# DeltaNet attention with a gated feed-forward on one core: the first block inverse in blocks of 8, joined on TensorE

## The chip, the cores and the metric

One core of one Trainium2 chip. The metric is the device time of one execution in microseconds; the median of the runs is given. Lower is better.

## The reference

A DeltaNet layer (4 batches, 8 heads, 768 positions, head dimension 48) is followed by a feed-forward block of width 2048 on the 3072 x 384 result. Cut to what matters:

```python
k_n = k / (norm(k) + 1e-6)
for t in range(S):                      # 768 steps, per batch and head
    y[:, :, t] = q_t @ state
    v_old = state^T k_t
    state += beta_t * outer(k_t, v_t - v_old)
x = y.transpose(0, 2, 1, 3).reshape(3072, 384)
h = x @ w_in                            # 384 x 2048
out = (h / (1 + exp(-1.702 * h))) @ w_out
```

The weights `w_in` and `w_out` and the inputs come as they are generated; the weights are 64-bit floats and are turned into fp32 on the chip.

## The kernel before, in words

**Chunks and units.** The sequence is cut into chunks of C = 128. Within a chunk the recurrence is a unit lower triangular system: with G = -K K^T and a scaling by beta, the new values U solve (I + N) U = V, block by block. There are 24 units (a chunk of a batch each, the later ones two half chunks of 64); units 0 to 3 are chunk 0 of the four batches, units 4 to 7 the next chunk, and so on. A unit holds all eight heads.

**The first inverse.** `diagonal(n)` makes the 32 x 32 diagonal blocks of N of unit n in PSUM (`psD`), scales them by beta (`bT`) on VectorE and leaves them in `XBs`. A transpose on VectorE (32 x 32 streams) puts all 128 blocks of the four units on 128 lanes (`NT`, one block to a lane). `invert(0)` inverts on VectorE the two 16 x 16 halves of each block, row by row: fifteen times a product and a reduction (`P`, `YB`), then a scaling by `bI` and a transpose back to `XBs`. `merge` makes a 32 x 32 inverse out of the two 16s on TensorE: `psP` = G times the lower half, a mask (`upper`) on ScalarE, `psZ` = the upper half plus the transposed inverse times it.

**Hops.** With the 32 x 32 inverses a unit is solved in four blocks: `solve` (`psU` = inverse times V), `below` (its product with G is added to `psV` for the later blocks), `rest` (copy of the next block of `psV` into V). Two units go in turn, `hops(a, b)` with `together`, nine steps for a pair. Then `put_out` makes the outputs (`psY`), the state `ST` and the rows `xT` of the feed-forward; `copies` sends the rows that lie across partitions through `last` and DMAs to `xT`.

**Weights.** Each piece of raw 64-bit words is fetched by DMA to spare places (`raw`, gT tiles, TW, the not yet used parts of `w_out`) and converted by five VectorE operations and one on ScalarE, the clamp (`conversion`, line 253 on). `fill(us)` puts as many microseconds of such conversions into VectorE's program order as its argument says; `background` continues behind the sixth `w_out` piece with `invert(1)`, the full inverse of units 4 to 7 on VectorE (lines 647 to 731), and then the rest of `w_out`. `invert(1)` begins with `NT` times `bL`: NT comes from `load_diagonals` (blocks of G, written to DRAM by `send_blocks`, read back), bL from sixteen small DMAs on POOL's queue. Its result goes through DRAM (`Yd`) back to `XBs`.

**Order.** What goes through `vec`, `act`, `pe`, `pool`, `sync` and `other_queue` (POOL's DMA queue) keeps the order in which it stands in the program (line 139, the line that the profile names for nearly all); each engine runs its instructions in order. `warm(n)` puts n products of a constant on TensorE that nobody reads. The order around the change is written out by hand in lines 1423 to 1620: all four `gram(b)` (G of units 0 to 3), `run(invert(0))`, the scores (`scored`, `psQ`) of units 0 to 2, `merge` and hops of units 0 and 1, then `merge` and hops of units 2 and 3 with one step of `hidden` (three products `ph`) at each hop (`feed`), then 25 rounds of `fill(1.0)` and `feed` that also norm the keys of units 8 to 11 (`normalize_mixed`: `ssq`, `rn`), then `slot(n)` for units 3 on, the loop that has the rest of the time. Pieces of `w_in` are fetched in step with the work (`paced`: a copy of a value into the target makes the DMA wait for that value).

Of the kernel before, what the change touches and what calls it, by code (L numbers as in the profile page):

```python
# [8 lines left out]
F32 = mybir.dt.float32  # L9
# [9 lines left out]
def kernel(  # L19
# [31 lines left out]
    NB = C // BS  # L51
    HB = 2
# [35 lines left out]
    YB = cpool.tile([128, BS, BS], F32, name="YB")  # L88

# [280 lines left out]
    def background():  # L370

        converting = conversions()
        while ("out", order[HF - 2]) not in done:
            yield next(converting)
        yield from invert(1)
        done.add("inverse")
        yield from converting
# [46 lines left out]
    def normalize_first():  # L424

        tt, add = vec.tensor_tensor, ALU.add
        z = wk.tile([128, 4, B, H], F32, tag="ksq", name="z", bufs=1)
# [128 lines left out]
    def diagonal(n):  # L556
# [6 lines left out]
        for j in range(NP):  # L563
            for k in range(NB):
                t = slice(k * BS, (k + 1) * BS)
                for hh in range(2):
# [4 lines left out]
                    )  # L571
        for hh in range(2):
            vec.tensor_tensor(
                XBs[:, n, hh::2], ps[hh],
                bT[:, n * H + hh : (n + 1) * H : 2].broadcast_to([128, NP, BS]), op=ALU.mult,
            )

# [68 lines left out]

    def invert(c, b0=0, nb=B):
# [4 lines left out]
        bc = (bL[part, c - 1] if c else bI[part]).broadcast_to([np, BS, BS])  # L652
        tt, red = vec.tensor_tensor, vec.tensor_reduce
        if c > 0:
            tt(N, N, bc, op=ALU.mult)
            yield 1.2
# [30 lines left out]
        if c > 0:  # L687
            X1 = N[:, 0:HS, HS:]
            turned = halves(Y)[1].rearrange("p l i -> p i l")
            vec.tensor_copy(X1, turned)  # L690
            A = N[:, 0:HS, 0:HS]
            N10, Y0 = N[:, HS:, 0:HS], halves(Y)[0]
        for j, Q in ((0, 2), (2, 2), (4, 4), (8, 4), (12, 4)) if c > 0 else ():
# [8 lines left out]
        for i, Q in ((0, 4), (4, 4), (8, 4), (12, 2), (14, 2)) if c > 0 else ():  # L702
# [10 lines left out]
        if c == 0:  # L713
            vec.transpose(by_lanes(XBs), YS.rearrange("p j i -> p i j"))
            for b in range(B):
                inverse[b] = XBs[:, b]
            return
# [16 lines left out]
    def merge(pair, area, banks):  # L734

        XT, Pm = (
            [area[:, a + i * n : a + (i + 1) * n].rearrange("p (h k) -> p h k", h=H) for i in range(HB)]
            for a, n in ((0, H * BS), (HB * H * BS, H * BS // 2))
        )
        Z, HS = [inverse[X.n] for X in pair], BS // 2  # L740
        rows = [slice(k * BS, (k + 1) * BS) for k in range(NB)]
        for X, t in zip(Z, XT):
            vec.transpose(t.rearrange("p h k -> p (h k)"), X.rearrange("p h k -> p (h k)"))
        for X, x, m in zip(pair, Z, Pm):
            ps = banks[0][0].tile([128, H, HS], F32, tag=banks[0][1], name="psP")
            for h in range(H):
                for r in rows:
                    pe.matmul(
                        ps[r, h, :], lhsT=X.G[r, h, r], rhs=x[r, h, HS:], start=True, stop=True,
                        skip_group_check=True,  # L750
                    )
            act.activation(m, ps, ACT.Copy, scale=upper)
            yield
        for x, t, m in zip(Z, XT, Pm):
            ps = banks[1][0].tile([128, H, HS], F32, tag=banks[1][1], name="psZ")
            pe.matmul(ps, lhsT=ident, rhs=x[:, :, HS:], start=True, stop=True, skip_group_check=True)
            for h in range(H):
                for r in rows:
                    pe.matmul(
                        ps[r, h, :], lhsT=t[r, h, :], rhs=m[r, h, :], start=False, stop=True,  # L760
                        skip_group_check=True,
                    )
            act.copy(x[:, :, HS:], ps)
            yield

# [8 lines left out]
    class Step:  # L774
# [17 lines left out]
        def scores(self):  # L792
# [17 lines left out]
            for g in range(0, NP, 2):  # L810
                pool_, tag = (ps_seq, "seq") if g else (ps_big, "big")
# [33 lines left out]
        def below(self, blk, h, psR):  # L845
            r = slice(blk * BS, (blk + 1) * BS)
            for k in range(blk + 1, NB):
                u = slice(k * BS, (k + 1) * BS)
# [4 lines left out]

        def rest(self, blk, psR):
            u = slice((blk + 1) * BS, (blk + 2) * BS)
            act.copy(self.V[u], self.psV[u])

        def solve(self, blk, h, psU):
            r = slice(blk * BS, (blk + 1) * BS)
            pe.matmul(  # L860
                psU[r, h, :], lhsT=inverse[self.n][r, h, :], rhs=self.V[r, h, :],
                start=True, stop=True,
            )

        def solved(self, blk, psU):
            r = slice(blk * BS, (blk + 1) * BS)
# [422 lines left out]
    def together(solves, belows):  # L1289
# [4 lines left out]
        psRs = [bank("psR") if X.n >= B else None for X, blk in belows]  # L1294
# [91 lines left out]
    for blk in range(NB):  # L1386
        sync(out=bI[blk * NBH : (blk + 1) * NBH], in_=betas[:, 0, blk, :])
    pool.memset(YB, 0.0)
    pool.affine_select(
        out=YB, in_=YB, compare_op=ALU.not_equal, fill=1.0, base=0,  # L1390
        pattern=[[1, BS], [-1, BS]], channel_multiplier=0,
# [13 lines left out]
    for b in range(B - 1):  # L1405
        load(b, ((QP, q),), sync)
    warm(NW)
    normalize_first()
    vec.transpose(bT, bI)
    upper = cpool.tile([128, 1], F32, name="upper")  # L1410
    vec.tensor_reduce(
        upper, ident.rearrange("p (k o i) -> p k o i", k=NB, o=2)[:, :, 0], axis=AX.XY, op=ALU.add
# [8 lines left out]
    vec.transpose(NT.rearrange("p i k -> p k i"), by_lanes(XBs))  # L1421
    pool.tensor_copy(home(B)[0:1, 0, 0:1], XBs[0:1, B - 1, H - 1, 0:1])
    for n in range(B, 2 * B):
        load(n, ((KN, k),), sync)
    load(B - 1, ((QP, q),), sync)
    for b in range(HB):
        load_values(b, sync)
# [232 lines left out]
```

## Time and profile before

| | |
|---|---|
| median of 3 runs | 692.75 us (686.65 to 693.12) |
| the profiled execution, its own time | 683.09 us |
| its span, mean granted TensorE clock | 681.4 us, 0.991 |
| TensorE (PE) busy | 660.4 us, 97% |
| VectorE (DVE) busy | 479.5 us, 70% |
| ScalarE (ACT) busy | 233.6 us, 34% |
| GpSimd (POOL) busy | 269.4 us, 40% |

| place in the profiled execution | us from the span's start |
|---|---|
| first inverse on VectorE, with its transposes | 21.68 to 38.17 |
| `merge` of units 0 and 1, first `psP` | 38.74 |
| hops of units 0 and 1 | 45.47 to 64.8 |
| hops of units 2 and 3 | 78.66 to 97.1 |
| `load_diagonals` of units 4 to 7, issue | 86.17 to 89.72 |
| `invert(1)` on VectorE | 103.06 to 134.26 |
| first `psU` of the slot loop | 153.83 |

How to read it: times are microseconds from the span's start; busy shares are averages over the whole span, and TensorE's share counts the unread products of `warm` too. In the page's slices each of the 40 columns is 17 us and each digit the busy share in tenths. In the chain of waits each row is a start, a duration and what the end of the program was waiting for in that time.

### The profile page before, as it was taken

How to read it: one execution, taken by the hardware profiler on the slowest of the kernel's cores; microseconds unless marked ns; L12 is line 12 of the kernel's file. 1: busy time of each engine (PE TensorE's matmuls, PEld its weight loads, DVE VectorE, ACT ScalarE, POOL GpSimd, SP SyncE). 2: the span in 40 equal slices, each digit the busy share in tenths (PEclk: the TensorE clock that was granted, in tenths of full speed). 3: DMA queues.
4: the chain of work that ended last, by engine and by line, in shares of the span. 5: the costliest groups of instructions: out<-in, count | busy, mean ns of one | idle time of the engine just before them, and what ended most of it. 6: DMA issues, size and time to landing. Idle time of an engine off the chain costs nothing.

```text
span 681.4 us, 21731 instructions
## 1 busy us (share of the span) xinstructions
PE 660.4 (97%) x9290; PEld 563.4 (83%) x9290; DVE 479.5 (70%) x890; ACT 233.6 (34%) x571; POOL 269.4 (40%) x282
## 2 busy tenths in 40 slices
PE   9899899799999999999999999999999999999997
PEld 4766678566678998998998988988988988989997
DVE  4889799983788997996997996997976970200000
ACT  2558463632333233333333233233233233322120
POOL 4032844320286634635535526426305205105041
PEclk9799999989999999999999999999999999999999
DMA  9567575263334435335335244244231130100101
GB/s 174 105 165 175 128 218 99 44 155 81 83 74 92 96 63 109 79 67 104 71 67 116 67 90 88 66 86 79 62 78 19 38 75 2 30 2 6 26 0 24
DMA packets 149632, 54.61 MB, mean 80 GB/s; under 512 B 137824, under 2 KB 142656, under 8 KB 149536
## 3 DMA queue, kind: packets, MB, share of 16 engines
q1 hardware_dynamic: 146368, 46.62, 32.7%
q0 software_dynamic: 3168, 6.61, 3.7%
q8 instruction: 73, 1.20, 0.8%
q14 instruction: 23, 0.19, 0.1%
HBM read 38.37 MB, written 13.63 MB: 76 GB/s over the span
## 4 chain that ended last, share of the span: by engine, by line
PE 86%; DVE 6%; ACT 2%; DMA 2%; issue 2%; SPq 1%; DVEq 0%; ACTq 0%
PE po L139 34%; PE ph L139 32%; PE four L139 7%; PE psU L139 3%; PE psR L139 2%; PE psG L139 2%; DVE P L139 2%; DVE w_out L139 2%; PE ps_warm L139 1%; DVE YB L139 1%; DMA TW<-in_q_dram 1%; PE psQ L139 1%; SPq L139 1%; PE psV L139 1%; DVE NT L139 1%
## 5 line engine op out<-in xcount | busy, mean ns | idle before, releaser
L139 PE MATMUL ph<-xT,w_in 128*128 128x256 f32 x1152 | 261.0, 384 | 2.3 <-ACT gT L139 2.0
L139 PEld LDWEIGHTS ph<-xT,w_in 128*128 128x128 f32 x1152 | 215.9, 190 | 33.8 <-ACT gT L139 2.4
L1118 POOL TENSOR_TENSOR gT<-gT 128x512 f32<-128x512 f32 x80 | 103.0, 1298 | 97.9 <-ACT gT L139 66.0
L139 PE MATMUL po<-w_out,gT 128*128 128x192 f32 (+1 forms) x720 | 138.4, 347 | 0.0
L139 DVE TENSOR_TENSOR P<-NT,YB 64x8 f32<-64x8 f32 (+13 forms) x195 | 124.8, 640 | 5.8
L139 PEld LDWEIGHTS po<-w_out,gT 128*128 128x128 f32 x720 | 118.5, 190 | 11.0 <-ACT o L139 0.5
L139 ACT ACTIVATE gT<-ph 128x512 f32<-128x512 f32 x90 | 53.8, 598 | 154.8 <-PE ph L139 154.8
L139 DVE TENSOR_REDUCE YB<-P 64x4 f32<-64x8 f32 (+13 forms) x195 | 78.4, 402 | 6.7
L139 PE MATMUL po<-TW,gT 128*128 128x192 f32 x480 | 81.8, 328 | 0.0
L139 PEld LDWEIGHTS po<-TW,gT 128*128 128x128 f32 x480 | 78.1, 190 | 0.7
L984 POOL TENSOR_SCALAR_AFFINE_SELECT M<-M 64x512 f32<-64x512 f32 x40 | 29.1, 727 | 90.0 <-ACT M L139 88.8
L139 DVE TENSOR_TENSOR o<-o,late 128x192 f32<-128x192 f32 x20 | 6.6, 356 | 68.1 <-ACT late L139 67.9
L139 ACT COPY VU<-psU 32x384 f32<-32x384 f32 x96 | 45.2, 470 | 21.3 <-PE psU L139 14.9
L139 DVE TENSOR_TENSOR VU<-VU,psR 32x384 f32<-32x384 f32 x40 | 22.1, 553 | 36.6 <-PE psR L139 35.9
L400 POOL TENSOR_TENSOR rn<-ssq,half 128x8 f32<-128x8 f32 x12 | 22.3, 1858 | 52.6 <-DVE ssq L139 52.6
L139 DVE TENSOR_TENSOR VU<-VU,four 128x384 f32<-128x384 f32 x19 | 10.4, 548 | 46.1 <-ACT M L139 46.0
L109 POOL DMA_DIRECT2D KN<-in_k_dram x24 | 17.2, 716 | 58.4 <-PE four L139 56.7
L139 ACT COPY o<-po 128x192 f32<-128x192 f32 (+1 forms) x44 | 14.7, 334 | 74.6 <-PE po L139 72.5
L139 PEld LDWEIGHTS psU<-VU,XBs 32*32 32x32 f32 x1536 | 27.4, 105 | 13.5 <-issue 8.5
L139 PE MATMUL psU<-VU,XBs 32*32 32x48 f32 x1536 | 32.6, 203 | 0.3 <-ACT VU L139 0.2
L139 DVE TENSOR_TENSOR P<-NT 64x512 f32<-64x512 f32 (+7 forms) x45 | 30.5, 679 | 1.1
L139 DVE TENSOR_REDUCE NT<-P 64x32 f32<-64x512 f32 (+9 forms) x45 | 30.0, 668 | 1.5
(167 smaller groups left out, 752.1 us busy)
## 6 DMA issues: line engine op xcount, KB each, us to landing
VU<-in_v_dram SPq DMA_DIRECT2D x40, 96.0 KB, 2.8
out_dram<-o SPq DMA_DIRECT2D x40, 96.0 KB, 2.2
QW<-in_q_dram SPq DMA_DIRECT2D x76, 48.0 KB, 2.2
Kd<-KN SPq DMA_DIRECT2D x56, 64.0 KB, 2.2
late<-Kd SPq DMA_DIRECT2D x14, 256.0 KB, 2.8
KN<-in_k_dram POOLq DMA_DIRECT2D x30, 96.0 KB, 3.1
w_out<-in_moe_w_out_dram SPq DMA_DIRECT2D x7, 384.0 KB, 3.8
NT<-Nd SPq DMA_DIRECT2D x20, 128.0 KB, 2.7
```

Source lines behind the costliest of these rows:

```text
L109: dma(out=place(dst, n)[rows, :, 0:D], in_=src[b, :, t, :].rearrange("h p d -> p h d"),)
L139: return lambda *a, **kw: tc.keep_in_program_order(op(*a, **kw))
L400: nc.gpsimd.tensor_tensor(rn, ssq, half, op=ALU.pow)
L984: nc.gpsimd.affine_select(out=M, in_=M, compare_op=ALU.is_gt, fill=0.0, base=0, pattern=[[0, H], [1, CH]], channel_multiplier=-1,)
L1118: (engine or nc.gpsimd).tensor_tensor(o, a, b, op=op)
```

## The change

- `diagonal` keeps only the 8 x 8 diagonal blocks: the product with beta goes through a mask (`bG`, beta times `in_eighth`) and a reduction over the four blocks of 8 of each 32. `invert_first` inverts the 8 x 8 blocks, four on a lane, in seven steps of a product and a reduction on 256 elements a lane; `spread` puts them back on the diagonal of 32 x 32 blocks.
- `merge` joins three times: 8 to 16, 16 to 32 (each `psP`, a mask, `psZ`), and 32 to 64 (`wides`, in NT). For units 0 and 1 (`first`) VectorE does the masks and sums of the level 8 and the sums of the level 16, for units 2 and 3 ScalarE.
- A unit is solved in two blocks of 64: `solve(0)`, `below`, `solve(1)`.
- Order of units 0 to 3: `gram` of each unit between the scores; values of units 0 and 1 are fetched before the keys of units 4 to 7; units 2 and 3 are merged and solved between steps of `hidden` (`pass_`); their values, the last third of the third quarter of `w_in` and its fourth quarter are fetched behind `put_out` of unit 1; the first `w_out` pieces (`fetch_out(0..2)`) behind the mask of unit 3; `turn` and `gram` of units 4 to 7, `load_diagonals` and the DMAs of `bL` behind the solves of units 2 and 3. Most `warm` calls go. `fill` arguments between the first inverse and the 25 rounds sum to 37 us instead of 49.

```diff
+    def invert_first():
+        tt = vec.tensor_tensor
+        vec.transpose(lanes_N.rearrange("p i k -> p k i"), by_lanes(XBs[:, :, :, 0:E8]))
...
+        for i in range(1, E8):
+            P = wk.tile([128, NE, i, i], F32, tag="P", name="P", bufs=1)
+            tt(
+                P, eighths(lanes_N, i * E8, [[0, i], [1, i]]), eighths(lanes_Y, 0, [[E8, i], [1, i]]),
+                op=ALU.mult,
+            )
+            vec.tensor_reduce(
+                eighths(lanes_Y, i, [[E8, i]]), P, axis=AX.X, op=ALU.add, negate=True
+            )
+        tt(lanes_N, lanes_Y, bI.broadcast_to([128, BS, E8]), op=ALU.mult)
+        vec.transpose(packed.rearrange("p n k -> p k n"), lanes_N.rearrange("p j i -> p i j"))
...
+        for s in (E8, 2 * E8):
...
+            turn_blocks()
...
+                        pe.matmul(
+                            ps[r, h, :], lhsT=X.G[r, h, r], rhs=o[r, h], start=True, stop=True,
...
+                if k == 1:
+                    act.activation(m, ps, ACT.Copy, scale=upper)
+                elif first:
...
+                        pe.matmul(
+                            ps[r, h, :], lhsT=t[r, h, :], rhs=m[r, h, :], start=first, stop=True,
...
+                if first:
+                    vec.tensor_tensor(o, o, split, op=ALU.add)
+                else:
+                    act.copy(o, split)
...
-        def below(self, blk, h, psR):
-            r = slice(blk * BS, (blk + 1) * BS)
-            for k in range(blk + 1, NB):
-                u = slice(k * BS, (k + 1) * BS)
+        def below(self):
+            r, u = slice(0, CH), slice(CH, C)
+            for h in range(H):
                 pe.matmul(
                     self.psV[u, h, :], lhsT=self.G[r, h, u], rhs=self.U[r, h, :],
...
+        def solve(self, blk):
+            r = slice(blk * CH, (blk + 1) * CH)
+            psU = bank("psU")
+            for h in range(H):
+                pe.matmul(
+                    psU[r, h, :], lhsT=wides[self.n][r, h, :], rhs=self.V[r, h, :],
...
+    put_out(pair[1])
+    scaling = roots_second(areas)
+    next(scaling)
+    merging = merge(pair[2:], area, ((ps_seq, "seq"), (ps_seq, "seq")), False)
+    fetch_in(2, js=(2,))
+    for b in range(HB, B):
+        load_values(b, sync)
+    for j in range(KC):
+        fetch_in(3, js=(j,))
...
+    def pass_(us=2.2):
+        feed()
+        fill(us)
...
+    run(scored[3])
+    pair[3].select()
+    fetch_out(0, other_queue)
+    fetch_out(1, other_queue)
+    fetch_out(2, other_queue)
...
+    put_out(pair[3])
+    pass_()
+    gram(B + 2)
+    turn(B + 3)
+    pass_()
+    Nds.append(send_blocks(B + 2))
+    gram(B + 3)
+    load_diagonals(Nds + [send_blocks(B + 3)])
+    done.add("diagonals")
```

## The prediction

> **What bounds the kernel now.** I read the page's slices first, then the chain of waits and the timelines of the first 160 us (none of the edits lies behind that), then the windows with the granted clock.
>
> ```profile
> PE   9899899799999999999999999999999999999997
> DVE  4889799983788997996997996997976970200000
> ```
>
> TensorE is full from slice 9 (153 us) to the end, so what is behind 153 us moves as a block. VectorE is full from slice 1 to 8 and has room in slice 9 (a digit of 3). The chain of waits over the first 160 us (start, duration, what):
>
> ```profile
> 82.79 3.72 DMA w_out<-in_moe_w_out_dram
> ...
> 103.06 1.23 DVE NT L139
> ...
> 131.38 0.21 DVE rn L139
> ...
> 136.84 1.73 PE psQ L139 x32
> ...
> 143.32 10.52 PE po L139 x32
> 153.83 0.80 PE psU L139 x32
> ```
>
> From 82.79 on the chain is VectorE: weight conversions, then from 103.06 the inverse of units 4 to 7, between whose steps stand the key norms `rn` that ScalarE and, behind it, TensorE wait for; from 136.84 TensorE alone. Call X the start of that inverse (103.06) and P the first `psU` of the slot loop (153.83). The change is worth what P moves, if nothing queues up behind it.
>
> VectorE's first inverse and the tail (start, duration, instruction):
>
> ```profile
> 21.68 2.06 DVE L139 STREAM_TRANSPOSE NT<-XBs 128x1024 f32<-128x1024 f32 x1
> ...
> 28.47 0.37 DVE L139 TENSOR_TENSOR P<-NT,YB 128x200 f32<-128x200 f32 x1
> 28.87 0.36 DVE L139 TENSOR_REDUCE YB<-P 128x20 f32<-128x200 f32 x1
> ...
> 36.08 2.09 DVE L139 STREAM_TRANSPOSE XBs<-NT 128x1024 f32<-128x1024 f32 x1
> ...
> 133.09 1.17 DVE L139 TENSOR_TENSOR NT<-YB,bL 128x1024 f32<-128x1024 f32 x1
> ...
> 154.57 0.56 DVE L139 SCALAR_TENSOR_TENSOR w_out<-raw,w_out 128x384 f32<-128x384 f32 x1
> ```
>
> **First inverse.** It holds VectorE from 21.68 to 38.17, 16.5 us. Afterwards: two transposes of 128x256 (a quarter of 2.06, 0.5 each), seven pairs of product and reduction over 4 to 196 elements (the rows for 2 to 200 elements take 0.16 to 0.37 each, with 0.04 between: 3.9), a scaling of 256 (0.42). With a reduction of 0.42 more per unit ahead of it (the last counts) it runs from 22.1 to 27.4; two spreads of 0.42 end at 28.3. TensorE is later: four products `psG` of 1.8 (7.21 for four), two transposes and sixteen `psQ`, all now ahead of the joins, end at 31.8.
>
> **Joins and hops of units 0 and 1.** Each of the levels 8 and 16 is four groups of 0.73 (the rows `psP`, `psZ` x64), with VectorE or ScalarE between (0.25 to 0.4 and 0.1 to wake): 3.3 us a level. Third level and wide copies: first `psU` at 41.7 (45.5 now). The trace has no 64x48 product, 64x32 join or copy of 32x256; the nearest rows (16 `psU` of 32 rows 0.86, copies of 128x256 0.37 and of 32x384 0.47) bound a group by 0.4 and 0.9, some 3 us over the whole chain; I take 0.45, since as many rows go through in half as many products. Three steps (solve, below, solve) of two to three us, with copies of 0.47, replace nine hops that take from 45.5 to 64.8; ScalarE copies the last state at 53.6 instead of 69.9. Sixteen us sooner, but that is not yet P: X needs VectorE.
>
> **VectorE's stream up to X.** From 38.06 to 103.06 it holds 55 us of work and 10 of waits. Joins and wide copies now end there at 40.2; behind that lie the same conversions (48.4 by their rows: 2.74 for a piece of 512, 2.25 of 384, 4.1 of 768), two more pairs of transposes, norms: 55.6 us, so X = 95.8 without waits. The order of the changed kernel shows these:
> - The third `w_in` piece (2,2) and the values of units 2 and 3 are issued on SP's queue behind the `xT` transfers that wait for 53.6: x3 about 2.3, x4 2.5, landing 4.3 later: 62.7, against 59.8 at which VectorE reaches it: 2.9. The values land at 63.5, and TensorE, in order, stands at `psV` from 57.5.
> - A clamp on ScalarE stands behind the first `ph` groups: 1.7.
> - The first `raw` transfers are issued on POOL behind the mask of unit 3, which waits for `psQ` at 76: select 1.1, issue 0.6, landing 4.0: 83.2 against 79.9: 3.3. Now they are issued at 60.0.
> - Pauses that the profile calls issue, as now: 3.
> Sum 10.9: X = 106.7. The work of units 2 and 3 on TensorE follows the values at 63.5: two `psV` 1.5, eleven `ph` groups of 1.33 (14.6), the level-16 and wide joins 5.5, `psQ` 1.2, six solves and belows of 0.45, four transposes 2.4, `psY` with states 2.7, four `psG` 2.8: 33, so `psG` of unit 7 ends at 96.
>
> **What X also waits for.** The beta transfers `bL` and the diagonals are queued as follows today:
>
> ```profile
> 71.93 9.31 POOL L139 DMA_DIRECT2D bL<-in_beta_dram  x16
> 86.17 3.55 SPq L139 DMA_DIRECT2D NT<-Nd  x4
> ```
>
> Today both are early. Now `bL` comes behind POOL's `xT` of unit 3 (94.7): 94.7 + 9.3 + 3.7 to landing = 107.7. The diagonals: G of unit 7 at 96.6, sent 1.8, landed 3.3, loaded and landed 4.5: 106.3. Queued behind that wait on VectorE are the inverse, three of the four `rn`, and the second half of `w_out`. X = 107.7, 4.6 later than now.
>
> **From X to P.** The inverse takes 31 us as now, so it ends at 138.9. Three chains: (a) its way through DRAM (Yd 2.2, issue, XBs 4.1) ends at 145.3, 8.4 before P; (b) TensorE: the four norms now stand earlier in VectorE's order, the last at 125.6 instead of 131.5 though X is later, `psQ` at 128.6, and 15.0 from there (16.9 now, less a `ph` group that is moved ahead and a pause) `psU` at 143.6; (c) the second half of `w_out`: its last conversion ends 52.0 after X now (155.1); the moved norms and the two VU rows give 0.6 back, so 159.1. TensorE uses it 12 us after P (165.75 today), 10.7 us of slack. (c) is last: P moves by 159.1 - 165.75 = -6.6. VectorE is then late by some ten us in the slot loop and has 18 us of idle time from 154 to 198 to catch up.
>
> **The clock.** The warm-up products between 28 and 78 us are taken out. Windows now (start:end, length, busy PE, PEld, DVE, ACT, POOL, granted clock, DMA share, GB/s):
>
> ```profile
> 16.00:20.00 4.00, 2.51 (x154) 1.98 (x140) 2.26 (x6) 1.74 (x3) 0.00 (x0) 1.00 0.38 54
> 20.00:24.00 4.00, 3.82 (x120) 3.65 (x96) 3.20 (x6) 1.08 (x3) 0.17 (x1) 0.61 0.13 25
> 24.00:28.00 4.00, 4.00 (x42) 4.00 (x40) 3.45 (x17) 2.45 (x5) 0.00 (x0) 0.54 0.68 127
> ```
>
> After four us of small tiles with a pause of 1.49 the clock falls to half. There 64 `psD` took 0.81 instead of 0.76, but sixteen products of 128 columns 1.8 (`psG`) instead of 1.16 (`psQ`). The joins of 31 to 51 are such small tiles: at half clock the wide products between (`psQ`, `psV`, `psY`) cost 2 us more, the `ph` behind the pause at 57.5 another 2. Price 0 to 4 (a gain is excluded, the clock is full there today); I take 1.6, for nearest are the joins today, at a clock of 1.00 with warm-ups among them.
> The Trainium skill, page "TensorE: Matmul & The Clock Gate", section Part 1, says that the clock is halved after an idle window of about 3.4 us and full after one of the same length busy. By that, only the pause at 57.5 (six us) costs, 2 us; the trace agrees behind the pause of 3.59 us at 133.2 (clock 0.79 from 136 to 144), not at 20 us, where 1.49 sufficed.
>
> **Without cost:** the small masks reduced from `ident` (VectorE idles 2.98 before 4.48; if not, 0.5), the moved memset of YB (POOL idles 12.77 before 21.71), the other bank of `psQ`, fewer paced signs (SP is issuing throughout).
>
> Forecast: P moves by -6.6 + 1.6 = -5.0. The profiled execution took 683.09 (span 681.4 and 1.7 around), 9.7 under the median of the runs shown; so 678.1 there, 692.75 - 5.0 = 687.8 as a median.
>
> **Rivals.**
> B, no waits on VectorE: values, raws and diagonals arrive as it reaches them, X = 103. Then (c) gives -11: 681.7. For it: all three transfers that I find late are late by 3 us only, and the row of VectorE before X shows such waits of 3.45 and 1.68 already. Against: three queues would have to be wrong in the same direction.
> C, late diagonals: landing times at the upper end (`raw` shows 3.7 to 6.5), a TensorE pause of 1.0 to 1.5 of kind issue in each of four stages: X = 114 to 118. (c) says 0 to +4: 693 to 697. P decides from X = 114.3.
> D, slower: the clock stays at half from 31 to 96 us, because joins keep breaking the `ph` groups. Twelve groups cost 1.33 more each, 16; four `psY` 1.3 each, 5: X = 129, +15: 707. It loses over 1% from X = 121. For it: the windows above. Against: from 64 to 104 the clock is 1.00 today with `ph` among small tiles and no warm-ups behind 74.
> That the change doesn't do what it says is excluded by the order of the instructions: seven pairs, three joins, solves of 64.
>
> **How the numbers follow.** Forecast 0.48 (its own range -8 to -1: 685 to 692), B 0.27, C 0.14, D 0.11. A measurement tells about 1%, 6.9 us. Faster by more: B and a seventh of the forecast, 0.33; slower: D and some of C, 0.14; within: 0.53. The range from 680 (B with 2 us of spread in the runs) to 698 (C's end) leaves out D and a tenth of B.
>
> **What would show it.** Right: VectorE idle ahead of `NT` with `bL` or `NT` as the releaser, X near 108; first `psU` near 42; TensorE idle at `psV` near 60; the last `w_out` conversion just ahead of its `po`. Wrong: X at 103 or less (B), `ph` groups of 2.6 at a clock of 0.5 before 96 us (D), P behind 154, or TensorE waiting in the slot loop for VectorE, which I count at nothing.

## The result, and the profile after

The changed kernel is slower: 719.5 us as the median of 4 runs (713.58 to 725.34) against 690.0 (686.65 to 693.12), a ratio of 1.04 with a 95% interval of 1.0299 to 1.0501. The ratio leaves out the longest run, 725.34 us, which counts as slow. The forecast was 687.8. The profiled execution has a span of 717.1 us and a mean granted clock of 0.946, before 681.4 and 0.991: 35.7 us more. The medians differ by 29.5 only. The profiled execution of the kernel before (683.09 us) is one of its quickest: the forty runs of it in the experiments below took 682.65 to 694.84 us at a clock of 0.989 down to 0.969, the longer in the main the lower. Some six of the 35.7 us are thus a matter of which execution was profiled.

The slices of the changed kernel (17.9 us a column):

```profile
PE   8869899988899999999999999999999999999997
...
DVE  5542764789868899799699798797995991110000
...
PEclk9655679999999999999999999999999999999999
```

The clock of the kernel before (17 us a column):

```profile
PEclk9799999989999999999999999999999999999999
```

VectorE, full from the second slice in the kernel before, is at 2 to 7 tenths up to 143 us. The clock is near half in the second to fourth slice (18 to 72 us), where it stood at full from the third slice on. The chain of waits of the changed kernel (start, duration, what):

```profile
18.03 2.32 issue
...
37.19 2.13 issue
...
41.23 2.38 issue
...
45.51 1.58 issue
...
58.31 3.59 PE psU L147 x32
...
65.00 3.58 PE psV L147 x32
...
69.62 3.58 PE psU L147 x32
...
83.75 3.63 DMA VU<-in_v_dram
...
134.60 0.69 PE psG L147 x32
...
139.69 3.59 DMA KN<-in_k_dram
```

Up to 135 us it is no longer VectorE's chain: joins, solves and `ph` groups on TensorE follow each other, with pauses and one wait for values between. Then come the diagonals and the keys of unit 8 behind them on SP's queue, and X. (As in the prediction, X is the start of the inverse of units 4 to 7 and P the first `psU` of the slot loop.) On VectorE (start, duration, instruction, idle time before it):

```profile
59.59 1.10 DVE L147 SCALAR_TENSOR_TENSOR w_in<-w_out,w_in 128x768 int32<-128x768 int32 x1 [6.23 <-ACT w_in L147]
...
71.11 0.96 DVE L147 SCALAR_TENSOR_TENSOR w_in<-w_out,w_in 128x768 int32<-128x768 int32 x1 [7.24 <-ACT w_in L147]
...
144.56 0.55 DVE L147 TENSOR_REDUCE ssq<-ksq 128x8 f32<-128x384 f32 x1 [2.81 <-ACT ksq L147]
...
145.91 2.01 DVE L147 TENSOR_TENSOR NT<-NT,bL 128x1024 f32<-128x1024 f32 x1
```

X is 145.91, before 103.06, forecast 107.7. P, the first `psU` of the slot loop, is 184.11, before 153.76: 30.35 us later. The other 5.4 of the 35.7 come behind P: the next slot's `psU` stands 20.3 us after P, not 14.9. TensorE pauses there for a copy on ScalarE and for the last `w_out` conversion, and twelve `po` take 5.83 us and not 4.14:

```profile
190.64 0.27 PE L147 MATMUL psR<-VU,G 32*32 32x48 f32 x2 [1.60 <-ACT VU L147]
...
201.45 3.04 PE L147 MATMUL po<-w_out,gT 128*128 128x384 f32 x8 [1.27 <-DVE w_out L147]
```

One row each, from 28 us to P, first before, then after (columns as in the prediction):

```profile
28.00:153.76 125.76, 112.76 (x1904) 84.65 (x1901) 114.16 (x212) 69.54 (x174) 51.48 (x62) 0.99 0.61 142
```

```profile
28.00:184.11 156.11, 136.64 (x2195) 110.76 (x2194) 100.14 (x195) 68.20 (x175) 48.25 (x57) 0.79 0.49 107
```

TensorE's busy time has grown by 23.9 us although 12.8 us of warm-ups are gone; VectorE's has shrunk by 14. This stretch holds most of the loss, and the experiments are read by its sum.

### The profile page after: what moved, and what is told of

The parts are those of the page before. It is cut to its first block, busy times and chain, and to the rows that moved or that the text cites. A ratio compares the mean times of both kernels' runs of the same rounds, so it can differ in the third digit from the quotient of the medians.

```text
span 717.1 us, 22298 instructions
## 1 busy us (share of the span) xinstructions
PE 684.7 (95%) x9560; PEld 588.3 (82%) x9560; DVE 477.4 (67%) x902; ACT 234.0 (33%) x575; POOL 268.9 (38%) x282
## 4 chain that ended last, share of the span: by engine, by line
PE 85%; issue 5%; DMA 3%; DVE 3%; POOL 2%; SPq 1%; ACT 1%; POOLq 0%; ACTq 0%; DVEq 0%
PE ph L147 32%; PE po L147 29%; PE four L147 7%; PE psU L147 4%; PE psG L147 2%; PE psR L147 2%; PE psV L147 2%; PE psP L147 2%; DMA raw<-in_moe_w_out_dram 1%; DMA KN<-in_k_dram 1%; PE psZ L147 1%; SPq L147 1%; PE psT L147 1%; PE psQ L147 1%; PE psY L147 1%
## 5 line engine op out<-in xcount | busy, mean ns | idle before, releaser
L147 PE MATMUL ph<-xT,w_in 128*128 128x256 f32 x1152 | 264.1, 387 | 3.4 <-ACT TW L147 2.4
L147 PE MATMUL po<-w_out,gT 128*128 128x192 f32 (+1 forms) x720 | 140.3, 350 | 1.3 <-DVE w_out L147 1.3
L147 PEld LDWEIGHTS po<-w_out,gT 128*128 128x128 f32 x720 | 119.1, 191 | 13.6 <-DVE w_out L147 1.9
L147 DVE TENSOR_TENSOR P<-NT,YB 64x512 f32<-64x512 f32 (+24 forms) x180 | 118.7, 660 | 5.1
L147 ACT ACTIVATE gT<-ph 128x512 f32<-128x512 f32 x90 | 53.6, 597 | 152.6 <-PE ph L147 152.5
L147 DVE TENSOR_REDUCE YB<-P 64x4 f32<-64x8 f32 (+26 forms) x180 | 73.5, 408 | 6.2
L1091 POOL TENSOR_SCALAR_AFFINE_SELECT M<-M 64x512 f32<-64x512 f32 x40 | 29.5, 738 | 86.3 <-ACT M L147 85.0
L147 ACT COPY VU<-psU 32x384 f32<-32x384 f32 (+1 forms) x88 | 41.4, 470 | 18.2 <-PE psU L147 16.4
L147 DVE TENSOR_TENSOR VU<-VU,psR 32x384 f32<-32x384 f32 x40 | 22.1, 554 | 32.5 <-PE psR L147 31.8
L147 DVE TENSOR_TENSOR P<-NT 64x512 f32<-64x512 f32 (+14 forms) x52 | 32.3, 621 | 1.9 <-DVE NT L147 0.5
L147 DVE TENSOR_REDUCE NT<-P 64x32 f32<-64x512 f32 (+16 forms) x52 | 31.7, 610 | 1.8
L147 ACT COPY xT<-four 128x256 f32<-128x256 f32 (+1 forms) x40 | 13.1, 328 | 42.7 <-PE four L147 42.7
L147 PEld LDWEIGHTS psU<-VU,XBs 32*32 32x32 f32 x1280 | 15.7, 105 | 8.1 <-issue 6.4
```

What stands on the lines that cost most here:

```text
L147: return lambda *a, **kw: tc.keep_in_program_order(op(*a, **kw))
L1091: nc.gpsimd.affine_select(out=M, in_=M, compare_op=ALU.is_gt, fill=0.0, base=0, pattern=[[0, H], [1, CH]], channel_multiplier=-1,)
```

## The experiments

**The theories.** Theory 1: the half clock makes TensorE's chain long. Theory 2: the chain of joins and 64-row products is long in itself. Theory 3: late transfers. They were named ahead of the first run; Theories 4 (the order), 5 (VectorE's idle time), 6 (one chain in which all add up), 7 (VectorE runs dry) and 8 (the place of the diagonals) came as the earlier ones fell. All runs named below but one (timed once) were timed in rounds against the kernel before, whose medians lay between 690.5 and 692.0. The changed kernel's own runs span 12 us, so its variants between 713 and 724 us are hardly told apart by their times. What the text says of their parts is read from one trace of each.

### The four first suspects

Warm-ups back between joins and solves:

```diff
-    for _ in range(2 * HB + 2):
-        next(merging)
+    for _ in range(HB + 1):
+        next(merging), next(merging)
+        warm(NM)
...
+    warm(NM // 2)
```

> The changed kernel with unread warm-up products put back between the joins and the solves of units 0 and 1 (some 9 us of products at full clock, most of it in pauses of TensorE). Theory 1, the clock: the half clock from 24 to 76 us is what made the chain long; the granted clock is above 0.9 in most of 28 to 76 us, the 32 psU products take 2.0 us and not 3.65, the start of the inverse of units 4 to 7 moves from 145.9 to 128-134 us and the time falls by 12 to 18 us (to 702-708). Theory 2, the serial chain: the clock is higher, but the added products and the waits for VectorE and ScalarE eat it; the inverse starts at 140 us or later and the time falls by less than 6 us. Theory 3, late transfers: the inverse starts within 3 us of 145.9.

Measured: 722.7 us, ratio 1.0441 (1.0363 to 1.0518); X 153.99. The clock was 0.50 from 48 to 64 us all the same: 17.5 us of warm-ups (1.0 in the changed kernel) did not hold it. This tells nothing of the clock's price.

No warm-ups in the kernel before:

```diff
-    NW, NR, NA, NY, NM, NU = 80, 11, 3, 14, 8, 12
+    NW, NR, NA, NY, NM, NU = 80, 11, 0, 0, 0, 0
...
+        if n == 0:
+            return
```

> The kernel before without any warm-up products behind the first ones. Theory 1: the granted clock falls to 0.5 from about 24 to 60 us or longer here too, and the kernel is slower by 6 to 15 us. Theory 2: the joins and hops of 32 rows cost nearly the same at half clock (64 psD took 0.81 against 0.76 us), so the time stays within 3 us of the kernel before, whatever the clock. Theory 3: no change.

Measured: 685.1 us, ratio 0.9937 (0.9904 to 0.9971): a little faster than the kernel before, and so the fastest of all. The two profiled executions, with spans of 681.4 and 682.4 us, do not show it, since that of the kernel before had a clock that none of its timed runs reached. From 28 us to P of this kernel:

```profile
28.00:154.80 126.80, 113.68 (x1845) 90.02 (x1845) 113.95 (x210) 68.20 (x172) 52.54 (x62) 0.87 0.63 141
```

The clock is at half from 40 to 64 us. TensorE's own work grows from 98.9 (112.76 less 13.84 of warm-ups) to 113.7, just what the warm-ups had taken, and P moves by 1.0. In these two executions of the old order half clock and warm-ups cost the same.

Hops of 32 for units 0 and 1 in the changed kernel, without their third join:

```diff
+        if first:
+            return
...
-    for X in pair[:2]:
-        X.solve(0)
+    hop((p0, 0), None, 0)
+    for i in range(NB - 1):
+        hop((p1, i), (p0, i), 0)
+        hop((p0, i + 1), (p1, i), 0)
```

> The changed kernel, but units 0 and 1 are solved in hops over four blocks of 32, as before, and their third join (32 to 64) is left out; units 2 and 3 keep blocks of 64. Theory 2, serial products of 64 rows: the third join (four groups of 3.6 us and the wide copies, some 14 us in all) goes, first psU comes at 45 to 49 us instead of 58.2, nine hops take some 20 us against 20 for the solves and belows of 64, so the inverse of units 4 to 7 starts 8 to 14 us sooner and the time falls by 8 to 14 us (to 706-712) although the clock stays at half. Theory 1: the clock stays at half, hops at half clock are slow as well, and the time falls by less than 5 us. Theory 3: less than 3 us.

Measured: 718.4 us, ratio 1.0401 (1.0328 to 1.0473), X 145.51. First `psU` comes at 53.2, five us sooner, and nothing is left of it at X: the hops at half clock, with copies between, take back what the join gave. (A pair has eight hops in the program, not nine.) In the new order the size of the blocks is not it.

Transfers early (bL to the front of POOL's queue, values of units 2 and 3 ahead of the first inverse, `fetch_out(0..2)` behind `put_out` of unit 1):

```diff
+        load_values(b, sync)
     invert_first()
...
+    fetch_out(0, other_queue)
```

> The changed kernel with transfers moved ahead: the sixteen bL loads to the front of POOL's queue, the values of units 2 and 3 ahead of the first inverse, the first three w_out pieces right behind put_out of unit 1. Theory 3, late transfers: the waits for VU (3.7 us), raw (2.25) and what stands behind them go; the inverse of units 4 to 7 starts 6 to 10 us sooner and the time falls by 6 to 10 us. Theories 1 and 2: these waits were short and other waits of the chain take their place; the time falls by 0 to 4 us.

Measured: 719.5 us, ratio 1.0429 (1.034 to 1.0519), X 145.03. Taken alone, Theory 3 falls: with the values there, TensorE's products with them (`psV`) start at 89.5 us, no sooner (87.4 in the changed kernel).

### The two halves of the change

The first inverse in blocks of 8 with the joins to 32, put into the kernel before, its order kept:

```diff
-    run(invert(0))
+    invert_first()
+    spread(0, 2)
+    spread(2, 2)
...
+    for _ in range(2 * HB):
+        next(products)
```

> The kernel before with the first inverse in blocks of 8 and the joins 8 to 16 and 16 to 32 alone: its order of units 0 to 3, its hops of 32, its warm-up products and its early transfers stay. Theory 4, the order: what costs is that the new order puts VectorE (by the clamps on ScalarE) and the diagonals behind the whole TensorE chain of units 0 to 3; here they are ahead of it again, so the inverse of units 4 to 7 starts at 95 to 104 us, the loop at 146 to 155 and the time is from 8 us under to 2 us over the kernel before. Theory 2, the serial chain: two more joins of 64 small products for each pair, with the masks and pauses between, put the chain late in any order: the first hop comes at 50 us or later, units 2 and 3 6 us later again, and the time is 8 to 15 us over the kernel before.

The same with the third join and blocks of 64 for all four units:

```diff
+    run(products)
...
+        if i % 2 == 0:
+            together(*next(path))
...
+        if i == 6:
+            load_diagonals(Nds)
```

> As the run with the first inverse alone, and with the third join and the solves over blocks of 64 for units 0 to 3, still in the order of before; the wide inverses lie in NT, so that the diagonals of units 4 to 7 are loaded only behind the last solve of units 2 and 3. Theory 4: the inverse of units 4 to 7 starts at 100 to 112 us, the time is from 6 us under to 6 us over the kernel before. Theory 2: serial products of 64 rows make the chain long whatever the order: the inverse starts at 120 us or later and the time is 15 to 28 us over the kernel before, near the changed kernel.

The first of these two without warm-ups:

> The first inverse in blocks of 8 in the old order with hops of 32, without the warm-up products behind the first ones. Theory 4: the chain of TensorE of units 0 to 3 is not what VectorE waits for, so the half clock costs within 2 us of the same kernel with warm-ups, or gains up to 6 us as it did in the kernel before. Theory 1, the clock: 6 to 15 us slower than with warm-ups.

And the new order with the inverse of before, one join, and hops of 32 for all units:

```diff
-    invert_first()
+    run(invert(0))
...
-        for s in (E8, 2 * E8):
+        for s in (2 * E8,):
```

> The new order alone: the first inverse of before (two 16 x 16 halves on VectorE), one join to 32 and hops of 32 for all four units, in the order, with the transfers and without most of the warm-ups of the changed kernel. If the order costs by itself (Theory 4): the inverse of units 4 to 7 starts at 125 us or later and the time is 12 to 25 us over the kernel before. If what costs is the longer chain of joins and 64-row products on TensorE and the order only passes it on (Theory 2): the inverse starts at 105 to 115 us and the time is within 8 us of the kernel before.

Measured:

| | order of before | new order |
|---|---|---|
| inverse of before, hops of 32 | 690.0 | 721.5, ratio 1.0437 (1.0361 to 1.0514) |
| blocks of 8, hops of 32 | 704.2, 1.0224 (1.0133 to 1.0316) | 718.4, 1.0401 (1.0328 to 1.0473); 64 in units 2 and 3 |
| blocks of 8, blocks of 64 | 714.7, 1.0326 (1.0226 to 1.0426) | 719.5, 1.04 (1.0299 to 1.0501) |

Without warm-ups the left middle is 704.7 (1.0218, 1.013 to 1.0307): the same, so Theory 1 (6 to 15 us slower) fell there. Each half costs by itself, the order most, and they do not add: in the new order blocks of 8 and 64 change little either way. In the old order the inverse in blocks of 8 starts X at 122.84 and not 103.06. Theory 4 put it at 95 to 104 and fell there. In the old order Theory 2 came true: its 8 to 15 and 15 to 28 us over the kernel before were 12.2 and 22.6. But it put the order alone within 8 us of before and fell there.

What holds TensorE in the order alone, from 28 to 150 us (waited for, us in total, times, longest):

```profile
PE psU L147 <- ACT VU L147: 8.7, 8, 1.5
PE psV L147 <- DMA VU<-in_v_dram: 5.4, 1, 5.4
PE psP L147 <- DVE XBs L147: 5.0, 1, 5.0
```

In the old order `turn` and `gram` of units 4 to 7 and warm-ups stood between the hops; without warm-ups its list has a single wait of `psU` for VU, of 0.2 us. In the new order only two groups of transposes stand between the hops of units 0 and 1, and five of the seven steps behind the first wait for ScalarE's copy, 4.6 us in all.

### The sum from 28 us to P

All kernels by one sum: P less 28 us is TensorE's own work, its warm-ups and its idle time (us; busy time by the window of each kernel, warm-ups by their tile).

| kernel | P | own work | warm-ups | idle |
|---|---|---|---|---|
| before | 153.8 | 98.9 | 13.8 | 13.0 |
| before, no warm-ups | 154.8 | 113.7 | 0 | 13.1 |
| blocks of 8, old order | 175.1 | 112.7 | 18.3 | 16.0 |
| blocks of 8, old order, no warm-ups | 174.3 | 125.7 | 0 | 20.7 |
| blocks of 8 and 64, old order | 187.6 | 124.5 | 17.4 | 17.8 |
| order alone | 185.6 | 124.0 | 1.0 | 32.6 |
| changed | 184.1 | 135.6 | 1.0 | 19.5 |
| changed, dense warm-ups (below) | 179.5 | 115.4 | 20.7 | 15.4 |
| changed, no join to 16 (below) | 180.7 | 131.2 | 1.0 | 20.5 |

P's 30.35 us are 36.7 more of own work, 12.8 less of warm-ups, 6.5 more of idle time. Of the 36.7, `psP` and `psZ`, the joins, are 17.7 (12.9 + 12.3 against 3.1 + 4.4).

The kernel before without warm-ups is the fairer base, since it too ran in part at half clock, and its profiled execution (684.08) lies 1.0 under its median. Against it the order alone has 10.3 us more of own work, 1.0 of warm-ups and 19.5 of idle time; the changed kernel has 21.9, 1.0 and 6.4. So the order alone costs most in waits. By these sums the longer work of the changed kernel fills much of what is idle time there, which fits that the two halves do not add.

### What VectorE waits for, and what the clock costs

In every kernel so far X less VectorE's idle time from 30 us on was 91 to 98 us (before 103.06 - 5.3, changed 145.91 - 52.3). Theory 5 made the idle time the cause. The clamp taken off ScalarE for the pieces ahead of the inverse:

```diff
-        act.activation(p, p, ACT.Relu, scale=8.0, bias=low)
+        if "inverse" in done or "late" in done:
+            act.activation(p, p, ACT.Relu, scale=8.0, bias=low)
+        else:
+            ts(p, p, 896 * E1, 896 * E1, op0=ALU.max, op1=ALU.subtract)
+            ts(p, p, 8, None, op0=ALU.mult)
```

> The changed kernel with the clamp of every weight piece that is converted ahead of the inverse of units 4 to 7 done on VectorE in two operations (about 10 us more of work there), not on ScalarE. Theory 5, VectorE's idle time: in all kernels run so far the inverse starts at 91 to 98 us plus VectorE's idle time from 30 us on (5.3 us in the kernel before, 52.3 in the changed one), and some 28 of the 52 us are waits for clamps that stand in ScalarE's order behind TensorE's work. With those waits gone the idle time falls to 15-30 us, the inverse starts at 122 to 136 us, and the loop starts 4 to 12 us sooner, since TensorE itself still needs about 45 us from psG of unit 7 (135) to the loop; the time falls by 4 to 14 us. Rival (Theory 2 alone): VectorE then waits for the joins and for transfers at the same places, the inverse starts within 5 us of 145.9 and the time changes by less than 3 us.

Measured: 723.9 us, ratio 1.0512 (1.0438 to 1.0586), X 149.77. The clamp waits are gone and others stand in their place:

```profile
75.15 0.95 DVE L147 TENSOR_REDUCE TW<-squares 128x16 f32<-128x768 f32 x1 [10.08 <-ACT squares L147]
...
118.15 0.36 DVE L147 TENSOR_SCALAR w_out<-raw 128x384 int32<-128x384 int32 x1 [9.40 <-DMA raw<-in_moe_w_out_dram]
```

VectorE's idle time shows how late TensorE's chain is; it is not the cause. Theory 5 falls.

Dense warm-ups between joins, solves and belows of units 0 and 1:

```diff
+        warm(ND)
...
+        warm(ND // 2)
```

> The changed kernel with so many warm-up products between the joins, solves and belows of units 0 and 1 (about 80 of 512 columns, 20 us at full clock, 40 at half) that the clock should stay full; it is meant to price the clock and not to be fast. Read: the time from the first psP to the last psY of unit 1 (34.3 to 78 us in the changed kernel, 44) less the busy time of the warm-ups. Theory 1: the rest is 24 to 30 us, since psU, psV and the 64-row joins take 2.0 us and not 3.6 and psY, psQ half. Theory 2: 34 us or more is left, in pauses and waits between the steps. If the clock stays at half all the same, warm-ups cannot hold it between these products and the question stays open.

Measured once: 713.2 us, 6.3 under the changed kernel's median and next to its lowest run (713.58), so that the time alone shows no gain. A window of this kernel and two rows of its chain of waits:

```profile
40.00:80.00 40.00, 38.42 (x917) 25.77 (x906) 19.35 (x35) 16.24 (x42) 3.95 (x7) 1.00 0.16 38
```

```profile
61.30 1.06 PE psU L147 x16
...
70.19 1.99 PE psU L147 x32
```

The clock is 1.00 from 40 to 80, and 32 `psU` take 1.99 us, not 3.58. By the expected reading, 36.1 to 76.4 us less 19.0 of warm-ups leaves 21.2, under the 24 to 30 of Theory 1 (the warm-ups also fill pauses). In the sum TensorE's own work falls by 20.2 us and the warm-ups cost 19.7: the clock is the largest single price in the changed kernel, and buying it back with warm-ups costs as much. With the clock held the joins take 20.1 us in all, not 25.2. What P gained, 4.6, is mostly idle time that they filled (19.5 to 15.4).

The join to 16 left out:

```diff
-        for s in (E8, 2 * E8):
+        for s in (2 * E8,):
...
-    for _ in range(2 * HB + 2):
+    for _ in range(2 * HB):
```

> The changed kernel without the join 8 to 16 of all four units (its two times four groups of products, masks and sums are left out, so the inverses lack those blocks). Theory 2, a serial chain: the join's length goes from the path twice: first psU at about 48 to 51 us and not 58.2, units 2 and 3 another 3 to 6 us, so psG of unit 7 is 10 to 16 us sooner, the inverse of units 4 to 7 starts 8 to 16 us sooner, the time falls by 8 to 16 us. Theory 3 or 5 with VectorE bound elsewhere: less than 4 us.

Measured: 714.2 us, ratio 1.0369 (1.0282 to 1.0456). The 5.3 us under the changed kernel are neither the 8 to 16 of Theory 2 nor clear of the runs' spread. First `psU` comes at 50.8, 7.4 sooner; X at 144.25, P at 180.73. Of 7.4 us in units 0 and 1, 3.4 reach P: TensorE then waits 5.5 us for the values of units 2 and 3.

Conversions moved to where VectorE idled in the old order:

```diff
+    fill(6.5)
...
-    fill(4.0)
+    fill(1.0)
```

> The kernel with the first inverse in blocks of 8 in the old order (hops of 32), with 9.5 us of weight conversions moved from behind the hops to where VectorE idled 8.05 and 9.06 us there: behind the first inverse and between the joins to 32. Theory 5: VectorE's idle time ahead of the inverse falls from 28.8 to about 15 us and the inverse starts at 108 to 116 us and not 122.8; the diagonals (landed at 112.8 us behind the TensorE chain) are then the floor; the time falls by 6 to 12 us against that kernel (to 0 to 9 us over the kernel before). Theory 2: the conversions only wait for the same transfers and joins; the inverse starts at 118 us or later, and the time falls by less than 4 us.

Measured: 720.7 us, ratio 1.0474 (1.0389 to 1.0559), 16.5 us over the kernel it was made from. The first wait behind the inverse:

```profile
42.88 0.69 DVE L147 TENSOR_SCALAR w_in<-w_out 128x768 int32<-128x768 int32 x1 [9.07 <-DMA gT<-in_moe_w_in_dram]
```

The second quarter of `w_in` is not there before 43 us, and what stands behind the wait in VectorE's order, the squares and masks of the joins, stands still with it: first `psP` at 56.5, not 40.1. Conversions could not use the time that the smaller inverse frees on VectorE, since with these transfers their data come later.

### Remedies together

Dense warm-ups, early transfers and early keys of units 8 and 9:

> The changed kernel with the dense warm-ups of the run before and all late transfers early: bL at the front of POOL's queue, values of units 2 and 3 ahead of the first inverse, the first three w_out pieces behind put_out of unit 1, keys of units 8 and 9 behind the last mask of units 2 and 3 and not behind the diagonals. Theory 6 (one serial chain through TensorE, SP's queue and VectorE, in which half clock and late transfers add up): the two gains add and the wait of 5.7 us for the keys of unit 8 goes too; the inverse of units 4 to 7 starts at 132 to 138 us, the loop at 170 to 176, the time falls to 702-709. Rival (TensorE's own stream behind psG of unit 7 sets the loop's start, some 49 us behind it): the inverse starts sooner, but the loop starts within 3 us of 179.5 and the time stays within 4 us of the dense warm-ups alone (713).

Measured: 713.4 us, ratio 1.0312 (1.022 to 1.0404), X 144.69, P 181.47: the rival's figures (P within 3 us of 179.5, the time within 4 of 713). Now the conversion of a piece of `w_in` waits for its transfer, and in VectorE's order the transposes for units 2 and 3 stand behind it (chain of waits):

```profile
82.36 8.51 DMA gT<-in_moe_w_in_dram
```

Weights early, `gram` of units 4 to 7 early, both, and all. In the kernels with early weights the first step of the conversion of piece (3,1) of `w_in`, its exponents, stands ahead of the transfer, so a twelfth of `w_in` comes out otherwise; the work is as much.

```diff
+    paced(XBs[0:1, 0, 0, 0:1], 2, 0)
...
-    def pass_(us=2.2):
+    def pass_(us=1.2):
...
+    for n in range(B, 2 * B - 1):
+        turn(n)
+        gram(n)
+        Nds.append(send_blocks(n))
```

> The changed kernel with its weights early: the pieces (2,1), (2,2) and (3,0) are fetched from the joins and first solve of units 0 and 1 on, the first three w_out pieces behind put_out of unit 1, the squares and roots of the keys of units 4 to 7 ahead of the solves, and 11 us of conversions are moved from the steps between the ph groups (2.2 to 1.2 each) into the joins and solves of units 0 and 1. Theory 7, VectorE runs dry: in the new order VectorE's program has some 10 us of conversions for a stage of 44 us of TensorE and DMA stands idle from 48 to 80 us; with this its idle time falls from 52 to 35-42 us. But the inverse still waits for the keys and diagonals behind psG of unit 7 (135), so it starts at 138 to 143 us and the time falls by 2 to 8 us. Rival: TensorE's chain sets all, psG of unit 7 and the start of the inverse stay within 3 us and the time within 3 us.

> The changed kernel with G and the diagonals of units 4 to 7 made ahead of the work of units 2 and 3 (three of them in the pause behind put_out of unit 1, the fourth behind the scores of unit 2; load_diagonals right behind the last solve of units 2 and 3). Theory 8, the place of the diagonals: the diagonals and the keys of unit 8 then land at about 128 us and not 143, some 8 us of idle TensorE between 78 and 87 us are used, and the inverse starts at 130 to 140 us; the time falls by 6 to 14 us. Theory 7: VectorE, dry in the first stage, still has its conversions to do, so the inverse starts at 140 us or later and the time falls by less than 5 us.

> Both: weights early with more conversions in the first stage, and G and diagonals of units 4 to 7 ahead of units 2 and 3. If the two are the two causes of the late inverse, each hides the other and together they give more than the sum: the inverse starts at 118 to 130 us, the loop 14 to 24 us sooner, the time falls by 12 to 24 us (695-707). If TensorE's own chain is the bound, it falls by less than 8 us.

> As the run with both, and with the dense warm-ups in the first stage and the values of units 2 and 3, bL and the keys of units 8 and 9 early. Adding the clock's 5 us: the inverse starts at 112 to 126 us and the time is 690 to 703. If the warm-ups only fill TensorE: no better than the run with both.

Measured:

| | us | ratio | X | P |
|---|---|---|---|---|
| weights early | 719.4 | 1.0392 (1.0346 to 1.0437) | 150.11 | 188.7 |
| grams early | 725.6 | 1.0484 (1.0444 to 1.0525) | 149.98 | 189.3 |
| both | 730.1 | 1.053 (1.0471 to 1.0589) | 160.08 | 197.7 |
| all | 717.5 | 1.0371 (1.0331 to 1.0412) | 145.59 | 182.0 |

None helped, and Theories 6, 7 and 8 fall. With all of them TensorE idles 10.5 us of the 154 from 28 us to P, and P is still 182: it has 121.8 us of own work and 21.7 of warm-ups to do. With grams early, `psG` of unit 7 comes 35 us sooner (99.5), the values' `psV` of units 2 and 3 13 us later (100.5) and the last `psY` of unit 3 4.4 later; X is then held by bL on POOL's queue, whose waits lie behind `put_out` of unit 3.

What stays open: how the 30 us of the order alone divide in cause, since its waits (hops 8.7, values 5.4, the inverse 5.0) and its longer half clock were not taken away one by one in that kernel. No run held the clock without paying for it, none brought the new order near the kernel before, and why the clock stays at half was not tried.

## Why the prediction was wrong

- **The first inverse**: 22.1 to 27.4 was forecast, with its two transposes; it runs from 23.26 to 29.41. The length (5.3 forecast, 6.15 measured) is near, since the transposes take 0.67 and not 0.5.
- **Joins and hops of units 0 and 1**: the step that failed. First `psP` 31.8 came at 34.3, first `psU` 41.7 at 58.2, the last copy of a state 53.6 at 79.3. `psG` of unit 7 is 39.3 us late at its end: 2.5 of them lie ahead of the joins, 14.0 in the joins of units 0 and 1, 9.2 in their solves and outputs, 13.6 behind the last state. The two added levels were eight groups of 0.73 and eight of 0.45, 9.4 us on TensorE; the joins took 17.7 more than before, and 12.6 more with the clock held. Sixteen products of 64x48 were bounded by 0.4 and 0.9 and taken at 0.45; at full clock they take 1.06 and at half 1.8, outside the bounds. Half of a 32-row group had no ground: a solve of 64 rows still has sixteen products, and each takes longer (66 ns at full clock) than one of 32 rows (49 ns, 0.79 us for sixteen).
- **The pauses in the joins**: 2.13, 2.38 and 1.58 us had no place in the chain. They stand inside groups of equal products, not between the steps: 128 products lie between the first and the second, 127 between the second and the third.
- **The clock**: the second term that failed. It was sized at 0 to 4 and taken as 1.6; TensorE's own work falls by 20.2 us when the clock is held. From 24 to 76 us of the changed kernel:

```profile
24.00:76.00 52.00, 45.26 (x862) 39.10 (x862) 22.82 (x51) 18.60 (x40) 2.54 (x4) 0.50 0.39 79
```

- Rival D, half clock from 31 to 96, came nearest, but half clock came from 24 to 76, ahead of the `ph` groups, and of the eleven up to `psG` of unit 7 only three took 2.8 us and the rest 1.5. D was priced at 15 us from the `ph` and `psY` groups alone. The joins, `psG`, `psQ` and solves ahead of them were left out.
- **VectorE's stream**: 55.6 us of work behind the joins was near: their last copy ends at 50.17 and not 40.2, X is 145.91, and 38.5 us between are waits, which leaves 57.2. (In the kernel before VectorE reads busy for 58.2 of the 65 us up to X, not 55.) The 10.9 of waits were these 38.5, since the times of TensorE from which they were taken were wrong. The waits for transfers were near the forecast (`w_in` 3.68 for 2.9, `raw` 2.25 for 3.3), but the clamps on ScalarE, forecast at 1.7, were 29.0. Values landed at 87.4, not 63.5.
- **What X waits for**: `psG` of unit 7 was forecast for 96 and ends at 135.3. That is 56 us behind the last copied state, where 42 were forecast (96 - 53.6). The sixteen bL issues start at 131.93 and X follows `psG` by 10.6 us (forecast 107.7 - 96 = 11.7): near. But the last wait ahead of X is for the keys of unit 8, whose transfer stands behind the diagonals, and not for bL or NT, which were named as its sign.
- **X to P**: P's own chains (a) and (b) were forecast to end 37.6 and 35.9 behind X; 38.2 measured. Near.
- **Behind P**: chain (c), the second half of `w_out`, was forecast to be last, and it is: TensorE was to use its last piece 51.4 us behind X (159.1 - 107.7) and does so 55.5 behind (201.45). TensorE's waits in the slot loop were counted at nothing; the way behind P is 5.4 longer.

So the links from X on were sound, and the start of the chain was mis-sized: TensorE's own work up to P is 135.6 us, 36.7 more than before, and the steps on record had added some eleven (9.4 of joins, 1.6 of clock). VectorE was indeed relieved (14 us less of busy time up to P), but with the work handed to TensorE the bound moved there. In the old order, too, blocks of 8 alone cost 2.2% (1.3 to 3.2).

## What to carry to other kernels

When work is moved from one engine to another that already reads 97% busy, sum the second engine's own work over the stretch up to the next meeting point, at the clock that this work itself will see, before counting what the first engine saves. Warm-up products that nobody reads are priced against the work that they speed up: in the profiled execution 13.8 us of them saved 14.8, and over the timed runs, most of which had a lower clock, the kernel without them was 0.6% faster. Where a profiled execution lies among its kernel's runs is looked up before two traces are subtracted. An order whose steps wait for each other across engines (clamps, masks, copies, transfers) is repaired by no single move: each remedy showed the next wait.

## What the runs showed of the hardware

The granted clock stayed at 0.50 from 24 to 76 us while TensorE was shown busy for 45.26 of the 52 us, and for all of the 12 us from 24 to 36. Most of it was joins of 32-row tiles and products of 48 or 64 rows. The Trainium skill, page "TensorE: Matmul & The Clock Gate", section Part 1, says that the monitor goes by how busy TensorE was in a window of about 3.4 us; the trace does not agree if busy is what the profile shows. From 40 to 64 us the clock was 1.00 with 12.7 us of dense 512-column warm-ups among the same groups, and 0.56 with 8.2 us of them.

Sixteen 64x48 products (one unit's solve, all on one half of the rows) took 1.06 us at full clock, 66 ns each, and thirty-two took 1.99. In the kernel before, 16 products of 32x48 on one row block took 0.79, 32 on two row blocks 0.80 and 64 on four 0.81: there the blocks ran beside each other.

The pauses of TensorE that the profile calls issue come at a fixed count. In the changed kernel 381, 128, 127, 507, 127 and 255 products lie from one to the next up to 99 us, each a multiple of 127 or 128 within three, and so in all the kernels; without the join to 16 the pauses at 41.23 and 45.51 are gone. The page of the changed kernel has the line

```profile
q8 instruction: 75, 1.23, 0.7%
```

which is 75 packets for 9560 products on TensorE, one for 127; in the kernel before 73 for 9290, the same. It looks as if each packet brought the code of 127 products with their weight loads, and as if the joins, which go through 128 products in 1.9 us, ran ahead of it: from one of the three pauses of the joins to the next it takes 4.3 and 3.5 us. This is inferred from the counts; no run was made for it.
